# Windowed attention feeding a routed expert layer: routing steps, gathers, buffers and weight loads re-timed

## The chip, the cores and the metric

The kernel runs on one core of a Trainium2 chip. The metric is the time of one execution in device microseconds (us); lower is better. The core has a matrix engine (TensorE, "PE"; its weight loads are listed apart as "PEld"), a vector engine (VectorE, "DVE"), a scalar engine (ScalarE, "ACT"), a general engine (GpSimd, "POOL"), an engine that here does nothing but start transfers (SyncE, "SP"), and 16 DMA engines that move the data. Each engine runs its own instructions strictly in the order in which they stand in its program, and waits at an instruction until everything that this instruction needs is there.

## What is computed

Attention with a sliding window (96 keys back, and 8 global keys at the start), 4 batches of 8 heads, 768 tokens, head size 64; its output, 3072 rows of 512, goes through a layer of 8 experts of which each token takes one.

```
# attention, per batch and head
scores = q @ k.T / sqrt(64) + bias(distance, head)
keep   = (pos_k < 8) | ((0 <= rel) & (rel < 96))
a      = softmax(where(keep, scores, -1e9));  out = a @ v
# x: (3072, 512), the heads side by side
logits = normalise(x) @ normalise(expert_emb).T / tau
e, gate = argmax(logits), softmax(logits)[argmax]
out[n] = gate[n] * (relu(x[n] @ w1[e[n]]) @ w2[e[n]])      # w1: 512x1024, w2: 1024x512
```

## The kernel before

The function `window_attention` (from L376) does the attention and, beside it, the routing: which expert each token takes and at which place of that expert's list of rows it stands. Two heads are one pair, so there are 16 pairs (4 in each batch), and each pair has two halves of 384 tokens. That makes 32 steps, one for each pair and half, counted from 0. Steps 0 to 23 are the first three batches, a pair's two halves one after the other. In steps 24 to 31 the last batch runs half by half: first half 0 of pairs 12, 13, 14 and 15, then half 1 of the same pairs.

A step s does the following, and PE, DVE, ACT and SP run it in the order in which the code is written. For POOL a scheduler sets the order when the program is built.

- `score`: 32 products of keys and queries on PE (L491), then `grow`, the exponential on ACT (L499, L504), and `weigh`, the multiplication with a table of the window and the bias on DVE (L514, L519).
- `turn`: transposes of the next pair's k and q on PE (L448) and copies of them on ACT.
- `turn_x`: the transpose of the finished rows `xs` of the step before on PE (L594), its copy to `xT` on DVE (L595).
- `attend` of step s-1: the products with v on PE (L562). `collect` of step s-1 on DVE: it divides by the sum (L571, L574) and writes into `xs`, a tile of 384 rows of 512 that four pairs fill. When a batch's half is full, `store_x` sends it to `x_dram` on SP (L579). There are three such tiles, used in turn.
- The values v of a pair lie in one of five tiles in turn. SP loads them (L472, L465), and a copy on POOL (L458, `spread_v`) puts the first 8 rows, the global keys, in place for every block. `attend` of the pair needs that copy. SP issues the loads of pair s//2+4: k and q at even s, v at odd s.

The routing of a batch (for the last batch, of each half) is a chain over several steps. `score_experts` (PE L612) and `turn_products` (PE L621, then DVE L622) give the logits `lg`. The generator `choose` then goes on in parts: on DVE the largest logit and the running counts (`m`, `oh`, `cum`, L200 to L212); on PE two small products that count over partitions (L218, L220); on DVE the totals (`both`, `cnt`, L227, L229), the norm (`ss`, L233 to L235), and place and weight of each token (`slot`, `gate`, `mt`, L241 to L255). POOL then scatters `mt` into the table `meta` in DRAM, 128 tokens for each indirect DMA (L259): six for a batch, three for a half. Batch 2 has its `score_experts` at the end of step 25, `turn_products` and the first DVE part in step 26, and the rest in step 27; half 0 of batch 3 has them in steps 29, 30 and 31. Half 1 of batch 3 is routed behind the last `attend`.

Expert 0's first 256 rows are taken from the first three batches, so that their products can start early: `first_rows` loads their entries of `meta` (SP L1011, the tile `emt`) after step 29 and waits for batch 2's scatters; `first_gathers` casts them to row numbers (POOL L683) and fetches the rows with two indirect DMAs (POOL L1021, `xg`) in step 31. `first_turn` transposes them (PE L692) and `first_product` multiplies them with w1 of expert 0 (PE L700).

SP also loads the weights of expert 0 in 32 pieces of 128 KB (L177, 16 of `w1t`, then 16 of `w2t`), from step 20 on: one in each step up to 22, then up to five. After the attention it loads 16 pieces of `w1t` of expert 1, the first of which waits for the gathers. Then it loads the entries of the next block of rows (`mts`, L1738), whose gathers (POOL L1021, `idss`) start the expert loop behind.

PSUM banks for all products but `od` are five tiles in a ring (`bank()`), so an instruction that takes a bank waits until the one five takes earlier is free.

Of the kernel before, what the change touches and what calls it, by code (L numbers as in the profile page):

```python
# [57 lines left out]
def build_route_consts(k):  # L58
    nc, pool = k.nc, k.const

    k.prefix = pool.tile([P, P], F32, name="prefix")
    nc.gpsimd.memset(k.prefix[:], 1.0)
# [4 lines left out]
    nc.gpsimd.iota(k.eidx[:], pattern=[[0, k.NT], [1, k.E]], base=0, channel_multiplier=0,  # L67
                   allow_small_or_imprecise_dtypes=True)
# [3 lines left out]
    nc.gpsimd.iota(k.fills[:], pattern=[[4, CAP // P]], base=0, channel_multiplier=0,  # L72
                   allow_small_or_imprecise_dtypes=True)
    k.wid = pool.tile([P, len(WIDTHS) - 1], F32, name="wid")
    nc.gpsimd.iota(k.wid[:], pattern=[[WIDTHS[-1] - WIDTHS[-2], len(WIDTHS) - 1]], base=WIDTHS[0],
                   channel_multiplier=0, allow_small_or_imprecise_dtypes=True)
# [3 lines left out]
    for i in range(2):  # L80
        nc.gpsimd.iota(k.tok[:, :, i], pattern=[[P, k.B * k.NT]], base=0, channel_multiplier=1,
                       allow_small_or_imprecise_dtypes=True)
    nc.gpsimd.tensor_scalar_add(k.tok[:, last:, 0], k.tok[:, last:, 0], 1.0)
    k.cnt = pool.tile([P, k.E], F32, name="cnt")
    nc.gpsimd.memset(k.cnt[:], 0.0)
    k.good = pool.tile([P, 1], F32, name="good")
    nc.gpsimd.memset(k.good[:], 1.0)
    zrow = pool.tile([P, k.DM // P], F32, name="zrow")
    nc.gpsimd.memset(zrow[:], 0.0)
    k.zrow = zrow  # L90
    k.fill = pool.tile([P, k.SL // P, 3], F32, name="fill")
    nc.gpsimd.memset(k.fill[:, :, 0], float(k.ZR))
    nc.gpsimd.memset(k.fill[:, :, 1], float(k.N))
    nc.gpsimd.memset(k.fill[:, :, 2], 0.0)
# [239 lines left out]
def window_table(k, tmp):  # L334
# [19 lines left out]
    nc.vector.tensor_scalar(out=t[:], in0=rel[:], scalar1=0.0, scalar2=None, op0=ALU.is_lt)  # L354
    yield
# [20 lines left out]
def window_attention(k, ctx):  # L376
# [17 lines left out]
    xt_p, xs_p, rt_p = pool("wa_xt", 2), pool("wa_xs", 3), pool("wa_rt", 2)  # L394
# [5 lines left out]
    values = [const.tile([P, 2, NB, D + 1], F32, name="v%d" % i) for i in range(5)]  # L400
# [42 lines left out]
    def turn(t, i):  # L443
# [5 lines left out]
        if i < 2:  # L449
            nc.scalar.copy(out=t.kT[:, 4 * half : 4 * half + 4, GLB:P],  # L450
                           in_=ps[:, 0:HALF].rearrange("d (j c) -> d j c", c=BLK))
        else:
            nc.scalar.copy(out=t.qT[:, half * HALF : (half + 1) * HALF], in_=ps[:, 0:HALF])
# [171 lines left out]
    def start_half(t, h):  # L625
# [4 lines left out]
        hf.count = 2 if t.b >= B - 2 else 3  # L630
        hf.last = hf.count + (t.b < B - 2)
# [17 lines left out]
    def half_ranks(hf):  # L649

        if hf.router and hf.phase == hf.count:
            hf.router.send(bank()[:, 3 * P :])
            next(hf.router)

    def half_root(hf):

        if hf.router and hf.phase == hf.last:
            next(hf.router)

    def half_router(hf):  # L660

        if hf.router and hf.phase in (1, hf.last):
# [3 lines left out]
        if (hf.t.b, hf.h, hf.phase) == (B - 2, 1, 2):  # L666
            k.base = k.const.tile([P, E], F32, name="base")
            nc.vector.memset(k.base[:], 0.0)
            nc.vector.tensor_scalar(out=k.base[:, 0:1], in0=k.cnt[:, 0:1], scalar1=float(FIRST), scalar2=None, op0=ALU.min)
# [11 lines left out]
    def first_gathers():  # L681
        ids = k.ea.tile([P, FIRST // P, 2], I32, name="ids", tag="ids")
        i = nc.gpsimd.tensor_copy(out=ids[:], in_=k.first.mt[:, :, 0:2])  # L683
        wait_for(k, i, k.root)
# [32 lines left out]
    load_tokens(nc.scalar, first.q, k.q, first, 0)  # L717
    idle = bank()
    nc.vector.memset(idle[:], 0.0)
    build_consts(k)  # L720
# [13 lines left out]
    for t in pairs[1:4]:  # L734
        open_pair(t)
        load_qk(t)
        if t is pairs[1]:
            load_v(first, True)
        load_v(t)
        if t is pairs[2]:  # L740
            emb = prep_expert_emb(k, k.emb_in, k.tau, tmp)
            next(emb)
# [3 lines left out]
    next(table)  # L746
    for v in values:
        nc.gpsimd.memset(v[:, :, :, D : D + 1], 1.0)
    for x in grown:
        nc.gpsimd.memset(x[:, :, :, 2 * BLK :], 0.0)  # L750
    for x in kept:
        nc.gpsimd.memset(x[:, :, BLK:], 0.0)
    next(numbers)
    next(table)
    build_route_consts(k)


    turn(first, 0)
    turn(first, 2)
    busy(1)  # L760
# [12 lines left out]
    for s, (g, p) in enumerate(steps):  # L773
# [6 lines left out]
        if ahead < len(pairs):  # L780
# [3 lines left out]
            else:  # L784
                load_v(pairs[ahead])
# [13 lines left out]
        grow(us[0], 1)  # L799
        if s == 0:  # L800
            turn(first, 3)
            next(table)
        scored = score(us[1])
# [5 lines left out]
        grow(us[1], 0)  # L809
# [14 lines left out]
        if waiting and (s >= 8 * (B - 1) or all(hf.phase >= 1 for hf in active)):  # L824
            active.append(start_half(*waiting.pop(0)))
        if s == len(steps) - 1:
            weigh(us[1])
        for hf in active:
            half_turns(hf)
        for x in whole_xs:  # L830
            turn_x(*x, nc.vector.tensor_copy)
        for hf in active:
            half_ranks(hf)
        if s == len(steps) - 1:
            gathers = first_gathers()
# [3 lines left out]
        weights_part(1 if s < drawn else 3)  # L839
# [14 lines left out]
        for hf in active:  # L854
            if hf.phase == 0:
                score_experts(hf)
            half_router(hf)
            hf.phase += 1
        if s >= len(steps) - 5:
            scatter_later(k, len(k.later))  # L860
# [7 lines left out]
    collect(*steps[-1])  # L868
    turn_x(*steps[-2], nc.scalar.copy)
    first_turn(0)  # L870
# [7 lines left out]
    first_turn(1)  # L878
# [969 lines left out]
```

## Time and profile before

| | us |
|---|---|
| median of 3 runs | 503.98 |
| lowest, highest | 503.79, 506.62 |
| profiled execution, its own time | 504.03 |
| its span, first to last instruction | 501.9 |
| steps 0 to 31 and the last attend, on PE | 6.98 to 158.45 |
| last half's routing and first rows, to the load of `mts` | 158.45 to 182.12 |
| expert loop and end | 182.12 to 501.9 |

The span is 2.1 us shorter than the time of the same execution, which has what lies around it. In the views that follow, a row of the timeline has the start, the duration of the group (us), the engine, the line, the operation, output<-input and how many; in brackets how long the engine stood idle ahead of it and what released it. A row of the waits has the total, the times and the longest, in us. A row of the windows has the stretch and its length, the busy time and number of instructions of PE, PEld, DVE, ACT and POOL, then the mean TensorE clock that was granted (1.00 is full), the DMA share and GB/s. Lines are those of the kernel before; the kernel after has the same code two or three lines further down in most places.

### The profile page before, as it was taken

To read this page: it belongs to the slowest core of one execution; us is meant where nothing else is said; L and a number is where in the kernel's file an instruction comes from. 1 tells how busy PE (TensorE), PEld (TensorE's weight loads), DVE (VectorE), ACT (ScalarE), POOL (GpSimd) and SP (SyncE) were. 2 spreads that over 40 slices of the span, in tenths; PEclk is the share of its full clock that TensorE was granted. 3 is DMA by queue.
4 is the path that set the end of the run, shared out by engine and by line. 5 is a ranking of instruction groups with operands and counts; after the bars stand their busy time and mean duration, and the time that the engine had idled before them with its cause. 6 is when DMAs were issued, how large, how long until landed. Compare 5 with 4: busy or idle time off the path is not lost.

```text
span 501.9 us, 12563 instructions
## 1 busy us (share of the span) xinstructions
PE 473.2 (94%) x4922; PEld 398.6 (79%) x4922; DVE 330.9 (66%) x686; ACT 177.8 (35%) x456; POOL 239.5 (48%) x287
## 2 busy tenths in 40 slices
PE   8899799999797997999999999999999999999995
PEld 6798688888586787879778578888899689869964
DVE  6677587887687555838575825976786765736631
ACT  5776666777663311302112212211221221311210
POOL 6121125225245224376568577666846726854022
PEclk9999999999999798999999999999999999999999
DMA  9999999998863737429561157265175175122001
GB/s 171 196 193 160 233 206 186 225 191 160 256 188 81 174 29 217 140 74 360 198 205 42 54 166 260 89 210 195 51 235 184 42 248 178 39 70 81 0 24 69
DMA packets 112636, 76.31 MB, mean 152 GB/s; under 512 B 88293, under 2 KB 96485, under 8 KB 112497
## 3 DMA queue, kind: packets, MB, share of 16 engines
q1 hardware_dynamic: 103632, 59.22, 47.3%
q0 software_dynamic: 8064, 15.27, 10.1%
q8 instruction: 60, 0.98, 0.9%
q14 instruction: 80, 0.65, 0.4%
q10 hardware_dynamic: 800, 0.20, 0.2%
HBM read 61.67 MB, written 17.16 MB: 157 GB/s over the span
## 4 chain that ended last, share of the span: by engine, by line
PE 69%; DVE 12%; issue 8%; DMA 5%; SPq 3%; POOL 2%; ACT 1%; DVEq 0%; POOLq 0%
PE big L1365 23%; PE big L1171 10%; PE work L1299 7%; PE od L562 6%; PE pa L491 4%; PE pa L700 3%; PE pa L448 3%; PE work L1312 3%; PE big L1342 2%; PE work L1171 2%; PE pa L594 2%; DVE xT L1057 1%; PE work L1090 1%; DVE ex L514 1%; PE pa L612 1%
## 5 line engine op out<-in xcount | busy, mean ns | idle before, releaser
L1048 POOL DMA_INDIRECT xg<-x_dram,squares x96 | 102.9, 1072 | 57.5 <-issue 41.7
L1375 DVE TENSOR_TENSOR hT<-big,hT 128x320 f32<-128x320 f32 (+4 forms) x70 | 39.0, 564 | 51.2 <-PE big L1365 44.8
L1365 PE MATMUL big<-xT,w1t 128*128 128x160 f32 (+4 forms) x336 | 59.4, 330 | 1.2 <-DVE xT L1109 1.2
L1365 PEld LDWEIGHTS big<-xT,w1t 128*128 128x128 f32 x336 | 54.8, 190 | 4.1 <-issue 2.1
L562 PE MATMUL od<-v,ex 128*64 128x65 f32 x1632 | 54.6, 224 | 0.0
L562 PEld LDWEIGHTS od<-v,ex 128*64 128x64 f32 x1632 | 50.3, 138 | 4.4 <-issue 4.2
L499 ACT ACTIVATE ex<-pa 128x384 f32<-128x384 f32 x96 | 42.2, 490 | 32.1 <-PE pa L491 31.8
L259 POOL DMA_INDIRECT meta<-mt,slot x24 | 26.7, 1114 | 46.7 <-PE pa L491 18.6
L491 PE MATMUL pa<-qT,kT 64*64 64x160 f32 (+3 forms) x1024 | 41.7, 288 | 2.1 <-issue 1.7
L1377 ACT ACTIVATE hT<-hT 128x320 f32<-128x320 f32 (+4 forms) x42 | 22.2, 531 | 59.4 <-DVE hT L1375 59.4
L514 DVE TENSOR_TENSOR ex<-ex,table 128x384 f32<-128x384 f32 x72 | 34.4, 519 | 11.8 <-ACT ex L499 10.3
L1365 PE MATMUL big<-xsum,fsum 128*128 128x160 f32 (+4 forms) x224 | 39.8, 331 | 2.1 <-DVE hT L1375 2.1
L491 PEld LDWEIGHTS pa<-qT,kT 64*64 64x64 f32 x1024 | 33.4, 135 | 9.5 <-issue 4.1
L1365 PEld LDWEIGHTS big<-xsum,fsum 128*128 128x128 f32 x224 | 36.4, 190 | 3.8 <-DVE hT L1375 2.6
L1318 POOL DMA_INDIRECT out_dram<-y_arm,tids x17 | 18.6, 1094 | 36.2 <-ACT y_arm L1301 23.7
L1299 PE MATMUL work<-w2t,hT 128*128 128x512 f32 x80 | 35.1, 594 | 0.0
L458 POOL COPY v<-v 32x896 f32<-32x896 f32 x15 | 15.5, 1036 | 37.0 <-DMA v<-in_v_dram 22.1
L519 DVE TENSOR_TENSOR ex<-ex,table 128x768 f32<-128x768 f32 x28 | 27.3, 974 | 9.0 <-ACT ex L499 8.7
L1171 PE MATMUL big<-wsum,hsum 128*128 128x256 f32 x136 | 31.1, 380 | 0.6 <-ACT ptmp L1197 0.5
L1171 PEld LDWEIGHTS big<-wsum,hsum 128*128 128x128 f32 x136 | 25.7, 190 | 5.1 <-issue 0.9
L1299 PEld LDWEIGHTS work<-w2t,hT 128*128 128x128 f32 x80 | 15.1, 190 | 17.6 <-issue 17.6
L1171 PE MATMUL big<-w2t,hT 128*128 128x256 f32 x112 | 27.6, 386 | 1.2 <-DVE hsum L1136 1.2
(240 smaller groups left out, 870.9 us busy)
## 6 DMA issues: line engine op xcount, KB each, us to landing
w1t<-in_moe_w_dram SPq DMA_DIRECT2D x24, 512.0 KB, 6.5
w2t<-in_moe_w_dram SPq DMA_DIRECT2D x6, 2048.0 KB
v<-in_v_dram SPq DMA_DIRECT2D x32, 192.0 KB, 5.5
x_dram<-xs SPq DMA_DIRECT2D x8, 768.0 KB, 6.4
k<-in_k_dram SPq DMA_DIRECT2D x30, 192.0 KB, 4.6
q<-in_q_dram SPq DMA_DIRECT2D x30, 192.0 KB, 5.5
w1t<-in_moe_w_dram SPq DMA_DIRECT2D x32, 128.0 KB, 6.2
w2t<-in_moe_w_dram SPq DMA_DIRECT2D x32, 128.0 KB, 3.3
```

The lines of the kernel that those rows point to most:

```text
L259: i = nc.gpsimd.indirect_dma_start(out=k.meta[:], out_offset=bass.IndirectOffsetOnAxis(ap=slot[:, t : t + 1], axis=0), in_=mt[:, t, :], in ...
L491: i = nc.tensor.matmul(u.sp[e][k0 : k0 + P // 2, x * 2 * BLK + c0 : x * 2 * BLK + c1], lhsT=t.kT[rows, j + x, k0 : k0 + P // 2], rhs=t.qT[ ...
L499: nc.scalar.activation(u.ex[:, e, :, 0 : 2 * BLK], u.sp[e][:, 0 : u.n].rearrange("p (x c) -> p x c", x=2), AF.Exp, scale=k.scale)
L514: nc.vector.tensor_tensor(out=to, in0=src, in1=tab, op=ALU.mult)
L519: nc.vector.tensor_tensor(out=ex, in0=ex, in1=tab, op=ALU.mult)
L562: nc.tensor.matmul(ps[g * SLICE : (g + 1) * SLICE, col : col + D + 1], lhsT=src, rhs=t.v[:, e, j, :], start=g not in begun, stop=True, ski ...
L1048: k.nc.gpsimd.indirect_dma_start(out=xgs[j][:, g * P : (g + 1) * P], out_offset=None, in_=src, in_offset=bass.IndirectOffsetOnAxis(ap=ids[ ...
L1171: i = self.k.nc.tensor.matmul(ps, lhsT=x[:, f, :], rhs=w[:, f, :], start=f == 0 and not add, stop=True, skip_group_check=True)
L1299: nc.tensor.matmul(ps[:], lhsT=hT[:, f, j * P : (j + 1) * P], rhs=w2[:, f, :], start=i == 0, stop=i == k.NF - 1)
L1365: nc.tensor.matmul(to[f // 2][:, f % 2 * 256 : f % 2 * 256 + h], lhsT=x[:, l, f * P : (f + 1) * P], rhs=y[:, l, 0:h], start=not (add or f ...
L1375: nc.vector.tensor_tensor(out=to, in0=x, in1=z, op=ALU.add)
L1377: nc.scalar.activation(to, to, AF.Relu)
```

## The change

It has five parts.

1. **Routing.** For batch 2 and half 0 of batch 3 (`hf.soon`) the first DVE part (`m` to `cum`) follows straight behind the last `xT` copy of the step, ahead of the step's second `weigh` and its `collect`. The two counting products on PE (L218, L220) stand at the end of that same step, behind `attend`, and no longer in the middle of the next one. The rest (`both` to `mt`) is issued in one go at the start of the next step (27, and 31), and the scatters there too, where they stood at its end. `turn_products` stands ahead of the `turn`s.
2. **First rows.** The load of `emt` stands after step 28, the gathers in step 30, both `first_turn`s right behind the last `attend`. A wait of the cast for the square root is taken out. `first_product(1, ...)` is cut after three columns and not after two.
3. **Buffers.** Four tiles of `xs` for three; four of v for five, with the loads of a pair's v issued one pair later.
4. **Weight pieces.** Five each in steps 23 to 25; the 14 that are left (`w2t` of expert 0) after the last `attend`, the first of them waiting for the gathers; then the last `store_x` and the 16 pieces of expert 1.
5. **Opening.** One memset and the constants change places and the memset covers fewer columns; the first copy of q goes from ACT to DVE; one more filler product; in step 0 the third exponential stands ahead of the table's; POOL's memsets and constants wait for an operation of the table on DVE; and SP issues k and q of pairs 1, 2, 3 with v of pairs 0, 1, 2 between them (v of pair 3 in step 1), so that one pair's v fewer lies ahead of the q of pair 2.

The core of the diff:

```diff
-    xt_p, xs_p, rt_p = pool("wa_xt", 2), pool("wa_xs", 3), pool("wa_rt", 2)
+    xt_p, xs_p, rt_p = pool("wa_xt", 2), pool("wa_xs", 4), pool("wa_rt", 2)
-    values = [const.tile([P, 2, NB, D + 1], F32, name="v%d" % i) for i in range(5)]
+    values = [const.tile([P, 2, NB, D + 1], F32, name="v%d" % i) for i in range(HP)]
...
+        hf.soon = t.b >= B - 2
+        hf.count, hf.last = (1, 2) if hf.soon else (3, 4)
...
         if hf.router and hf.phase == hf.count:
             hf.router.send(bank()[:, 3 * P :])
+            if not hf.soon:
+                next(hf.router)
+
+    def half_chain(hf):
+
+        if hf.router and hf.soon and hf.phase == 1:
             next(hf.router)
 
+    def half_slots(hf):
+
+        if hf.router and hf.soon and hf.phase == hf.last:
+            for _ in range(3):
+                next(hf.router)
...
-    for t in pairs[1:4]:
+    for i, t in enumerate(pairs[1:4]):
         open_pair(t)
         load_qk(t)
-        if t is pairs[1]:
-            load_v(first, True)
-        load_v(t)
...
+        load_v(pairs[i], not i)
...
+    signs = next(table)
...
+        wait_for(k, nc.gpsimd.memset(x, what), [signs])
+    build_route_consts(k, signs)
...
-            else:
-                load_v(pairs[ahead])
+        if s % 2 and ahead - 1 < len(pairs):
+            load_v(pairs[ahead - 1])
...
         grow(us[0], 1)
+        for hf in active:
+            half_slots(hf)
...
         if s < len(steps) - 5:
             scatter_later(k, 1, [scored] + k.root)
-        grow(us[1], 0)
+        else:
+            scatter_later(k, len(k.later))
...
         for hf in active:
-            half_ranks(hf)
+            half_chain(hf)
+            if not hf.soon:
+                half_ranks(hf)
+        if s == len(steps) - 2:
+            gathers = first_gathers()
...
-        weights_part(1 if s < drawn else 3)
+        if s < drawn + 3:
+            weights_part(1 if s < drawn else 5)
...
             if hf.phase == 0:
                 score_experts(hf)
+            if hf.soon:
+                half_ranks(hf)
             half_router(hf)
...
-        if s == len(steps) - 3:
+        if s == len(steps) - 4:
             first_rows()
-        weights_part(0 if s < drawn else 2)
...
     collect(*steps[-1])
+    for j, (e, i) in enumerate(weights):
+        wait_for(k, load_weights_part(k, e, k.w[e], i), [] if j else gathers)
...
     for i in range(PIECES // 2):
-        wait_for(k, load_weights_part(k, 1, k.w[1], i), gathers if i == 0 else [])
+        load_weights_part(k, 1, k.w[1], i)
```

How the instructions stand afterwards, at three places. First POOL, from batch 1's scatters (`mt_2013` before, `mt_2008` after) to the gathers. The v tiles are numbered: before, `v_109` is that of pair 15, the last; after, it is `v_112`. Before:

```order
L458 COPY v_112<-v_112 32x2x7x64
L259 DMA meta<-mt_2013,slot_2008 28672x3
L458 COPY v_113<-v_113 32x2x7x64
L259 DMA meta<-mt_2013,slot_2008 28672x3 x2
L458 COPY v_109<-v_109 32x2x7x64
L259 DMA meta<-mt_2013,slot_2008 28672x3
L223 TENSOR_TENSOR ss<-ss,half 128x6
L259 DMA meta<-mt_2527,slot_2522 28672x3 x6
L223 TENSOR_TENSOR ss<-ss,half 128x3
L683 CAST ids<-emt 128x4
L1021 DMA xg<-x_dram,ids 128x512 x2
```

The copy for pair 15 stands ahead of the last scatter of batch 1. After, on the same engine at the same place:

```order
L262 DMA meta<-mt_2008,slot_2003 28672x3 x2
L460 COPY v_111<-v_111 32x2x7x64
L226 TENSOR_TENSOR ss<-ss,half 128x6
L262 DMA meta<-mt_2468,slot_2463 28672x3 x6
L460 COPY v_112<-v_112 32x2x7x64
L697 CAST ids<-emt 128x4
L1044 DMA xg<-x_dram,ids 128x512 x2
```

The copy for pair 15 now stands behind all six scatters of batch 2 (`mt_2468`). Next PE, at the end of step 26 in the kernel after (`od` are the products of `attend`, L564; L493 are the scores of step 27):

```order
L596 MATMUL pa_127<-ident,xs 128x128 x3
L564 MATMUL od<-v_110,ex_115 64x65 x13
L564 MATMUL od<-v_110,ex_116 64x65
L564 MATMUL od<-v_110,ex_115 64x65
L564 MATMUL od<-v_110,ex_116 64x65 x9
L221 MATMUL pa_123<-oh,prefix 128x48
L223 MATMUL pa_123<-cum,ones 128x48
L493 MATMUL pa_124<-qT,kT 64x128
```

Before, the two counting products stood behind the `turn_x` of step 27, ahead of that step's `attend`; now they close step 26. Last, SP from the last v load to the load of `mts`, after:

```order
L474 DMA v_112<-in_v_dram 96x8x64 x2
L467 DMA v_112<-in_v_dram 32x2x64
L180 DMA w1t<-in_moe_w_dram 128x256 x3
L180 DMA w2t<-in_moe_w_dram 128x256 x2
L581 DMA x_dram<-xs 128x3x512
L1034 DMA emt<-meta 128x2x3
L180 DMA w2t<-in_moe_w_dram 128x256 x14
L581 DMA x_dram<-xs 128x3x512
L180 DMA w1t<-in_moe_w_dram 128x256 x16
L1761 DMA mts<-meta 128x4x3 x8
```

Before, all 16 pieces of `w2t` stood ahead of the load of `emt`; now 14 of them stand behind it, and the load of `emt` stands right behind the store of batch 3's half 0, as it did with one piece between.

More of the change, by code (lines that the diff above doesn't have):

```diff
@@ L452, in turn @@
         else:
-            nc.scalar.copy(out=t.qT[:, half * HALF : (half + 1) * HALF], in_=ps[:, 0:HALF])
+            copy(out=t.qT[:, half * HALF : (half + 1) * HALF], in_=ps[:, 0:HALF])
         if i == 0:
@@ L652, in half_ranks @@
             hf.router.send(bank()[:, 3 * P :])
+            if not hf.soon:
+                next(hf.router)
+    def half_chain(hf):
+        if hf.router and hf.soon and hf.phase == 1:
             next(hf.router)
+    def half_slots(hf):
+        if hf.router and hf.soon and hf.phase == hf.last:
+            for _ in range(3):
+                next(hf.router)
+            if hf.t.b == B - 2:
+                k.base = k.const.tile([P, E], F32, name="base")
+                nc.vector.memset(k.base[:], 0.0)
+                nc.vector.tensor_scalar(out=k.base[:, 0:1], in0=k.cnt[:, 0:1], scalar1=float(FIRST), scalar2=None, op0=ALU.min)
     def half_root(hf):
-        if hf.router and hf.phase == hf.last:
+        if hf.router and not hf.soon and hf.phase == hf.last:
             next(hf.router)
     def half_router(hf):
-        if hf.router and hf.phase in (1, hf.last):
+        if hf.router and not hf.soon and hf.phase in (1, hf.last):
             next(hf.router)
@@ L665, in half_router @@
             check_sums(hf.t)
[L666 to L669, printed above, removed]
     def first_base():
@@ L682, in first_gathers @@
         ids = k.ea.tile([P, FIRST // P, 2], I32, name="ids", tag="ids")
-        i = nc.gpsimd.tensor_copy(out=ids[:], in_=k.first.mt[:, :, 0:2])
-        wait_for(k, i, k.root)
+        nc.gpsimd.tensor_copy(out=ids[:], in_=k.first.mt[:, :, 0:2])
         xgs, gathers = gather_rows(k, ids, k.ea2, FIRST // P, k.ZR + 1)
@@ L717, in window_attention @@
     load_tokens(nc.scalar, first.q, k.q, first, 0)
+    build_consts(k)
     idle = bank()
-    nc.vector.memset(idle[:], 0.0)
-    build_consts(k)
+    nc.vector.memset(idle[:, 64:], 0.0)
     warm = const.tile([P, 1], F32, name="warm")
@@ L745, in window_attention @@
     table = window_table(k, tmp)
[L746 to L752, printed above, removed]
+    signs = next(table)
+    for x, what in ([(v[:, :, :, D : D + 1], 1.0) for v in values] + [(x[:, :, :, 2 * BLK :], 0.0) for x in grown] +
+                    [(x[:, :, BLK:], 0.0) for x in kept]):
+        wait_for(k, nc.gpsimd.memset(x, what), [signs])
+    build_route_consts(k, signs)
+    turn(first, 0)
+    turn(first, 2, nc.vector.tensor_copy)
+    busy(2)
     next(numbers)
     next(table)
[L755 to L760, printed above, removed]
     turns = [[] for _ in steps]
@@ L808, in window_attention @@
             scatter_later(k, 1, [scored] + k.root)
-        grow(us[1], 0)
+        else:
+            scatter_later(k, len(k.later))
+        if s:
+            grow(us[1], 0)
+        if waiting and (s >= 8 * (B - 1) or all(hf.phase >= 1 for hf in active)):
+            active.append(start_half(*waiting.pop(0)))
+        for hf in active:
+            if hf.soon:
+                half_turns(hf)
         todo = turns[s]
@@ L823, in window_attention @@
             emb.send(bank() if s == 7 else None)
[L824 to L827, printed above, removed]
         for hf in active:
-            half_turns(hf)
+            if not hf.soon:
+                half_turns(hf)
         for x in whole_xs:
```

64 lines of the change are left out of this document (32 added, 32 removed).

## The prediction

> **What bounds the kernel now.** I read the page's busy times first, then the waits of PE and DVE, then the timeline of the stretches that the change touches.
>
> ```profile
> span 501.9 us, 12563 instructions
> PE 473.2 (94%) x4922; PEld 398.6 (79%) x4922; DVE 330.9 (66%) x686; ACT 177.8 (35%) x456; POOL 239.5 (48%) x287
> ```
> ```profile
> PE pa L491 <- issue: 1.7, 1, 1.7
> ```
> ```profile
> DVE xs L574 <- DMA x_dram<-xs: 3.6, 1, 3.6
> ```
>
> PE is busy for 94% of the span, so what a part of the change is worth is the PE idle time that it takes away or brings. What happens on another engine counts only where PE waits for it. The profiled execution took 504.03 us, 0.05 over the median, and the sum is made against it. All positions below are on the clock of the kernel before.
>
> **A, opening: -1.4.** In step 2 PE waits for the q of pair 2 (first row). The new load order puts one pair's v less ahead of it.
>
> ```profile
> 19.81 0.52 PE L448 MATMUL pa<-ident,q 128*128 128x128 f32 x3 [1.65 <-DMA q<-in_q_dram]
> ```
> ```profile
> 12.00:16.00 4.00, 4.00 (x96) 3.50 (x96) 2.93 (x5) 3.97 (x14) 0.00 (x0) 1.00 1.29 187
> 16.00:20.00 4.00, 2.21 (x47) 1.66 (x42) 2.33 (x6) 3.04 (x8) 0.92 (x1) 1.00 1.27 197
> ```
> ```profile
> v<-in_v_dram SPq DMA_DIRECT2D x32, 192.0 KB, 5.5
> ```
>
> A pair's v is two transfers of 192 KB, 393 KB in all; at the 187 and 197 GB/s of those windows that is 2.0 to 2.1 us, more than the wait of 1.65, which goes. ACT is next late: from 12 to 16 it is busy for 3.97 of 4 us, and the exponential put ahead of the table's there can push a consumer by up to its own half microsecond; the q copy on DVE gives ACT as much back. I take +0.25 of that, and bounds of -1.9 to -1.0. POOL's memsets wait for DVE now, but POOL has nothing in 12 to 16, so I price that, the memset, the filler product and the moved constants inside these bounds. The v loads that come a pair later still come three pairs (six steps) ahead of use, against 5.5 us from issue to landing: nothing.
>
> **B, fourth `xs` tile: -3.0.** DVE stood at L574 for a tile that its store had not yet left, and PE stood behind it:
>
> ```profile
> 60.50 0.56 DVE L574 TENSOR_TENSOR xs<-od,rd 128x384 f32<-128x384 f32 x1 [3.58 <-DMA x_dram<-xs]
> ```
> ```profile
> 61.20 0.52 PE L594 MATMUL pa<-ident,xs 128*128 128x128 f32 x3 [2.63 <-DVE m L200]
> ...
> 66.26 0.52 PE L594 MATMUL pa<-ident,xs 128*128 128x128 f32 x3 [0.65 <-DVE xs L574]
> ```
>
> The two PE gaps are 3.28 us. With a fourth tile the store has a half batch more time; I leave 0.3 for what DVE itself is late with. Bounds -3.3 to -2.6.
>
> **C, batch 2's routing and POOL's order: +7.5.** This is the large term. DVE in steps 26 and 27:
>
> ```profile
> 132.97 0.56 DVE L595 COPY xT<-pa 128x384 f32<-128x384 f32 x1 [0.70 <-PE pa L594]
> 133.45 0.82 DVE L514 TENSOR_TENSOR ex<-ex,table 128x384 f32<-128x384 f32 x2
> ...
> 134.46 0.20 DVE L571 RECIPROCAL rd<-od 128x6 f32<-128x6 f32 x1
> ...
> 135.17 0.19 DVE L200 TENSOR_REDUCE m<-lg 128x6 f32<-128x48 f32 x1
> ...
> 136.56 0.97 DVE L212 TENSOR_TENSOR cum<-cum,oh 128x8 f32<-128x8 f32 x5
> ...
> 138.85 0.21 DVE L227 TENSOR_TENSOR both<-pa,cnt 128x56 f32<-128x56 f32 x1
> ...
> 139.17 0.82 DVE L514 TENSOR_TENSOR ex<-ex,table 128x384 f32<-128x384 f32 x2
> ...
> 140.18 0.17 DVE L233 TENSOR_SCALAR ss<-ss 128x6 f32<-128x6 f32 x1
> ...
> 140.73 0.19 DVE L571 RECIPROCAL rd<-od 128x6 f32<-128x6 f32 x1
> ...
> 141.43 0.20 DVE L241 TENSOR_TENSOR both<-both,oh 128x48 f32<-128x48 f32 x1
> ...
> 142.41 0.19 DVE L255 RECIPROCAL mt<-gate 128x6 f32<-128x6 f32 x1
> ```
>
> And PE:
>
> ```profile
> 132.79 1.62 PE L562 MATMUL od<-v,ex 128*64 128x65 f32 x48
> ...
> 137.58 0.42 PE L220 MATMUL pa<-cum,ones 128*128 128x48 f32 x2 [0.72 <-DVE cum L212]
> ...
> 142.10 1.62 PE L562 MATMUL od<-v,ex 128*64 128x65 f32 x48
> ```
>
> The `xT` copy of step 26 ends at 133.53. The chain from `m` to `cum` takes 2.36 (135.17 to 137.53), so `cum` is ready at 135.9. PE is done with that step's `attend` at 134.41 and waits 1.5 there; behind its wait stand the scores of step 27. In return step 27 loses the wait of 0.72, so the `attend` of step 28 would come at 142.10 + 0.8 = 142.9. On DVE `weigh` and `collect` of step 26 follow the chain (133.45 to 134.46 and 134.46 to 135.17, 1.72 in all), so `both` starts at 137.6. From `both` to the end of `mt` took 3.75 (138.85 to 142.60), of which 1.01 (`weigh`) and 0.70 (`collect`) stood between and do so no more: 2.04, `mt` at 139.65, three microseconds sooner than before. POOL then starts the scatters:
>
> ```profile
> 142.89 1.70 POOL L259 DMA_INDIRECT meta<-mt,slot  x1 [7.07 <-DVE base L669]
> ...
> 150.24 1.37 POOL L259 DMA_INDIRECT meta<-mt,slot  x1 [0.30 <-issue]
> ```
> ```profile
> 58.67 0.92 POOL L458 COPY v<-v 32x896 f32<-32x896 f32 x1 [8.01 <-PE pa L448]
> ```
>
> The six take 8.72 us (142.89 to 151.61), so they end at 148.4. By the new order of POOL the v copy of pair 15 stands behind them: 0.3 + 0.92 more, 149.6. `attend` of step 28 is the first to use this v, and PE waits there with everything behind it. Before, the copy stood ahead of a scatter of batch 1 and was long done. PE stands for 149.6 - 142.9 = 6.7 us, and with the 0.8 the term is +7.5; +6.5 if `mt` comes a microsecond sooner, +8.5 if later.
>
> **D, the clock behind that stall: +2.5.** A PE that stood still got half a clock afterwards:
>
> ```profile
> 163.00:171.00 8.00, 8.00 (x33) 5.55 (x34) 1.84 (x10) 3.13 (x8) 1.43 (x2) 0.61 0.74 154
> 196.00:200.00 4.00, 3.84 (x16) 3.87 (x17) 3.71 (x20) 0.30 (x1) 0.00 (x0) 0.57 0.72 209
> ```
>
> A mean of 0.61 over 8 us is 6.2 us at half (0.39 x 8 / 0.5); 0.57 over 4 is 3.4. A stretch at half clock loses half its length where PE sets the pace: 3.1 or 1.7. I take 2.5, with 0 and 3.4 as ends; 0 because the gap of 2.63 at 61.20 cost nothing, though 6.7 is far longer. The Trainium skill, "TensorE: Matmul & The Clock Gate", Part 1, has a rule that speaks against this change: an idle window of about 3.4 us halves the clock until a busy one has passed. By that rule a wait of 6.7 us all but surely holds such a window, the half clock lasts 3.4 to 6.8 us, and the term is 1.7 to 3.4; without the rule it could be nothing, and the sum would be 502.8.
>
> **E, the same wait at the end of step 30: +0.8.** Batch 3's half 0 has three columns, not six, so its chain is shorter. It lies between 0 and the 1.5 of step 26; I take the middle.
>
> **F and G, the end of the attention: -2.8 and -2.5.**
>
> ```profile
> 156.88 1.57 PE L562 MATMUL od<-v,ex 128*64 128x65 f32 x48
> ```
> ```profile
> 160.84 0.66 PE L692 MATMUL pa<-ident,xg 128*128 128x128 f32 x4 [1.91 <-DMA xg<-x_dram,ids]
> ...
> 162.83 1.12 PE L692 MATMUL pa<-ident,xg 128*128 128x128 f32 x4 [1.01 <-DMA xg<-x_dram,ids]
> 163.88 1.51 PE L612 MATMUL pa<-xT,enb 128*32 128x384 f32 x8
> ```
>
> PE waits 1.91 and 1.01 for the gathered rows. They come sooner than the attention's end in the new order (below), so both go, less 0.1 for the last `xs`: F -2.8, bounds -2.9 to -2.0. With the gap gone the clock stays full, and the 6.2 us at half behind it give back up to 3.1; I take G -2.5, because the logits' way over DVE does not get shorter, and 0 if the clock falls there all the same.
>
> **H and I, small ones: +0.3 and -0.6.**
>
> ```profile
> 181.93 1.89 PE L1171 MATMUL big<-w2t,fhT 128*128 128x256 f32 x8
> ```
>
> The weight pieces that now land while the first products run share the DMA engines with them; PE reads the `w2t` pieces from 181.93 on. I take +0.3, between 0 and 1.5. The wait of 1.7 us at L491 with no releaser may be gone when the code lies elsewhere, which I give a third: -0.6.
>
> **J, SP's queue behind the gathers: +0.5.** 30 pieces stand now between the gathers and the load of `mts`:
>
> ```profile
> 126.33 4.40 SPq L177 DMA_DIRECT2D w1t<-in_moe_w_dram  x5
> ...
> 144.87 0.39 SPq L579 DMA_DIRECT2D x_dram<-xs  x1
> ...
> 154.54 0.38 SPq L1011 DMA_DIRECT2D emt<-meta  x1
> ...
> 162.93 12.11 SPq L177 DMA_DIRECT2D w1t<-in_moe_w_dram  x16
> 182.12 4.86 SPq L1738 DMA_DIRECT2D mts<-meta  x8
> ```
>
> The load of `emt` stands behind the store of batch 3's half 0, which needs the `collect` of the stalled `attend`: 2.77 us after its start before (142.10 to 144.87), some 1.6 more at half clock, and the 0.4 of the store: 149.6 + 4.8 = 154.4. From the issue of `emt` to the landing of the gathers it was 8.3 (154.54 to 162.83): 162.7, and less A and B, 158.3 on the new clock. A piece took 0.757 us (12.11 / 16) or 0.88 (4.40 / 5), so 30 of them are done at 181.0 or 184.7. `mts` is due at 182.12 plus the other terms, about 183. So PE waits between nothing and 1.8 us more.
>
> **Sum:** -1.4 - 3.0 + 7.5 + 2.5 + 0.8 - 2.8 - 2.5 + 0.3 - 0.6 + 0.5 = +1.3, so 504.03 + 1.3 = 505.3. What is gained at three places is given back at one.
>
> **Rivals.**
>
> R1, no stall: the copy is through POOL before PE needs it, so C is +0.8 and D is 0. That is 505.3 - 6.7 - 2.5 = 496.1. For it: the order is a list and not a time, and the 8.72 us rest on one row of six scatters. Against it: POOL takes what stands first, and the scatters start only with `mt`. To be 1% faster the copy must end by about 145. Chance 0.13.
>
> R2, slower: SP's queue takes over. If the gathers land 2.2 us later than I say (160.5) and a piece takes 0.88, `mts` comes at 186.9, 3.9 later than due and, beyond the 0.5 already in, that is 508.7; with a landing where it was before (162.8) it is 511. Middle 509.8. It decides from a landing of about 159 at 0.88 a piece. For it: four steps hang one behind the other (stall, `collect`, store, `emt`). Against it: before, 16 pieces left SP idle for five microseconds ahead of `mts`. Chance 0.17.
>
> R3, the change doesn't do what it says: the loads set the attention's pace, so a wait taken out comes back at the next transfer, and A and B give nothing: 505.3 + 4.4 = 509.7. For it: a DMA share over 1 from 12 to 20. Against it: that falls behind the opening. Chance 0.05.
>
> **How the numbers follow.** The forecast has 0.65, its own range is 501 to 509.5: C by 1, D and G by up to 2.5 each, not all one way. R2 and R3 lie up to 511, R1 at 496.1. From 498.5 to 511 about 0.83 is held; R1's middle is left out. About 1% (5.0 us) can be told from no change. Under 498.9: R1 and a little of the forecast's lower end, 0.15. Over 509.0: two thirds of R2 and R3, and the upper end of the forecast, 0.18. Within: 0.67.
>
> **What would show it.** C: in step 28 PE idle for 5 to 8 us ahead of L564, released by POOL's copy behind six scatters. D: a clock of 0.5 for 3 to 7 us behind it. A and B: no wait for q in step 2, none for the store of `xs`, `score` of step 24 about 4.4 sooner than before. F, G: no wait for `xg` behind the last `attend`, and full clock there. J: SP goes from the last piece into the load of `mts` without idling. The prediction is wrong if PE does not stand in step 28, or if `mts` comes later than 185.

## The result

The changed kernel takes 509.14 us (median of 20 runs, 505.18 to 515.15), the kernel before 503.65 on the same chip (20 runs, 500.56 to 510.24). The ratio is 1.0105, 95% interval 1.0076 to 1.0133: slower by about 1%. The ratio is taken over the runs in the chip's faster state alone, so it is not exactly the quotient of the medians. The prediction said 505.3 with a range of 498.5 to 511.

The page of the changed kernel has a longer span, PE busy for a slightly smaller share of it, and a different chain of work that ended last. First three lines of the kernel after (span, busy times, the chain by engine), then the chain by engine of the kernel before:

```profile
span 508.1 us, 12564 instructions
PE 474.0 (93%) x4924; PEld 397.6 (78%) x4924; DVE 330.2 (65%) x687; ACT 177.4 (35%) x455; POOL 243.8 (48%) x286
PE 49%; issue 16%; DMA 13%; POOL 13%; DVE 4%; POOLq 2%; SPq 1%; ACT 1%; ACTq 0%; DVEq 0%
```
```profile
PE 69%; DVE 12%; issue 8%; DMA 5%; SPq 3%; POOL 2%; ACT 1%; DVEq 0%; POOLq 0%
```

PE works about as long as before (474.0 against 473.2), so 5.4 of the 6.2 us of span are waiting. On the chain POOL and DMA went from 2% and 5% to 13% each: the gathers that POOL issues stand on it. Most of that is not in step 28, where the prediction looked. The shares alone do not price anything, though: a version below that is faster than the kernel before (opening and buffers alone) has POOL at 17% and DMA at 11%.

Where the time stands on PE's clock in the two profiled executions (504.03 and 510.48 us):

| mark | before | after | difference |
|---|---|---|---|
| score of step 3 | 22.13 | 20.30 | -1.8 |
| score of step 13 | 68.63 | 63.52 | -5.1 |
| score of step 26 | 127.16 | 124.57 | -2.6 |
| end of the last attend | 158.45 | 162.76 | +4.3 |
| counting products of the last half done | 170.78 | 169.96 | -0.8 |
| load of `mts` | 182.12 | 185.21 | +3.1 |
| first 160-column product of the expert loop | 196.16 | 198.84 | +2.7 |
| first 192-column product | 373.51 | 374.36 | +0.9 |
| first 240-column product | 410.90 | 415.66 | +4.8 |
| last group of products | 494.20 | 500.46 | +6.3 |

Four stretches matter. In step 28 PE stops where the prediction said. PE's timeline of the kernel after, then POOL's, then the clock over the whole stretch and over the two microseconds in which it falls and comes back:

```profile
139.17 0.56 PE L564 MATMUL od<-v,ex 128*64 128x65 f32 x10
144.22 2.43 PE L564 MATMUL od<-v,ex 128*64 128x65 f32 x38 [4.49 <-POOL v L460]
146.58 2.03 PE L493 MATMUL pa<-qT,kT 64*64 64x128 f32 x32
```
```profile
135.55 1.31 POOL L262 DMA_INDIRECT meta<-mt,slot  x1 [3.94 <-DVE base L670]
...
142.27 0.96 POOL L262 DMA_INDIRECT meta<-mt,slot  x1 [0.30 <-issue]
143.23 0.94 POOL L460 COPY v<-v 32x896 f32<-32x896 f32 x1
```
```profile
136.00:150.00 14.00, 8.26 (x146) 7.27 (x144) 6.52 (x15) 4.03 (x15) 6.64 (x7) 0.76 0.32 77
141.00:142.00 1.00, 0.00 (x0) 0.00 (x0) 0.00 (x0) 0.00 (x0) 0.96 (x1) 0.79 0.04 5
148.00:149.00 1.00, 1.00 (x18) 0.90 (x11) 0.35 (x2) 1.00 (x4) 0.00 (x0) 0.79 0.57 215
```

The copy of pair 15's v runs behind the sixth scatter, and `attend` resumes as it ends. A mean clock of 0.76 over 14 us is 6.7 us at half. A mean of 0.79 in a microsecond is 0.42 us at half, so the clock falls at about 141.6, 1.9 us into the wait, and is back at about 148.4. Some 2.6 us of the half clock fall into the wait and the rest on work: the two groups behind the wait take 2.43 and 2.03.

At the attention's end the waits for the gathered rows are gone, and all is caught up:

```profile
161.01 1.75 PE L564 MATMUL od<-v,ex 128*64 128x65 f32 x48
162.82 0.55 PE L596 MATMUL pa<-ident,xs 128*128 128x128 f32 x3
163.20 1.04 PE L705 MATMUL pa<-ident,xg 128*128 128x128 f32 x8
164.08 0.49 PE L596 MATMUL pa<-ident,xs 128*128 128x128 f32 x3
164.50 1.55 PE L614 MATMUL pa<-xT,enb 128*32 128x384 f32 x8
```

No group has an idle time in brackets. Up to the counting products the change is ahead by 0.8 us. Then it loses. SP's and POOL's timeline of the kernel after, and the wait of SP's queue (in this part of the kernel the lines of the kernel after stand 23 further down: L1761 is L1738 before):

```profile
167.18 13.20 SPq L180 DMA_DIRECT2D w1t<-in_moe_w_dram  x16
185.21 4.55 SPq L1761 DMA_DIRECT2D mts<-meta  x8
```
```profile
175.84 0.96 POOL L262 DMA_INDIRECT meta<-mt,slot  x1 [0.30 <-issue]
189.04 1.25 POOL L1044 DMA_INDIRECT xg<-x_dram,idss  x1 [12.23 <-issue]
```
```profile
SPq L1761 <- DMA meta<-mt,slot: 3.6, 1, 3.6
```

SP is done with the pieces at 180.38 and then waits for the scatters, the last of which POOL had finished at 176.80. From there to the load of `mts` it is 8.4 us; before it was 4.7 (177.39 to 182.12). While the pieces move, the scatters land later. This reaches PE by way of DVE, which stands at the conversion of `mts` with a sum behind it (`hsum`) that PE needs. DVE and PE of the kernel after, then DVE of the kernel before at the same place, where PE did not wait:

```profile
188.06 0.17 DVE L1765 CAST idss<-mts 128x16 int32<-128x16 f32 x1 [5.13 <-DMA mts<-meta]
```
```profile
188.88 3.33 PE L1194 MATMUL big<-wsum,hsum 128*128 128x256 f32 x8 [2.12 <-DVE hsum L1156]
```
```profile
184.83 0.18 DVE L1742 CAST idss<-mts 128x16 int32<-128x16 f32 x1 [0.65 <-DMA mts<-meta]
```

Behind this wait of 2.12 the clock is at half for another 3.4 us (a mean of 0.76 from 187 to 194).

The last loss is far behind, in the expert loop. PE of the kernel after, and DVE at the same place:

```profile
374.36 2.76 PE L1388 MATMUL big<-xT,w1t 128*128 128x192 f32 x16
379.01 2.87 PE L1388 MATMUL big<-xsum,fsum 128*128 128x192 f32 x16 [1.89 <-DVE fsum L1158]
383.37 2.87 PE L1388 MATMUL big<-xT,w1t 128*128 128x192 f32 x16 [1.49 <-ACT hT L1412]
```
```profile
373.43 1.10 DVE L1080 STREAM_TRANSPOSE xT<-xg 128x512 f32<-128x512 f32 x1 [5.22 <-DMA xg<-x_dram,squares]
```

DVE waits 5.22 us for rows that a POOL gather brings, and PE for DVE. POOL's queue has fallen back: the first gather for these rows starts at 339.99 here and started at 323.86 before (next two rows, after and before), while PE is one microsecond apart.

```profile
339.99 0.99 POOL L1071 DMA_INDIRECT xg<-x_dram,squares  x1 [9.23 <-issue]
```
```profile
323.86 1.27 POOL L1048 DMA_INDIRECT xg<-x_dram,squares  x1 [3.49 <-issue]
```

### The profile page after: what moved, and what is told of

The parts are those of the page before. It is cut to its first block, busy times and chain, and to the rows that moved or that the text cites. A ratio compares the mean times of both kernels' runs of the same rounds, so it can differ in the third digit from the quotient of the medians.

```text
span 508.1 us, 12564 instructions
## 1 busy us (share of the span) xinstructions
PE 474.0 (93%) x4924; PEld 397.6 (78%) x4924; DVE 330.2 (65%) x687; ACT 177.4 (35%) x455; POOL 243.8 (48%) x286
## 4 chain that ended last, share of the span: by engine, by line
PE 49%; issue 16%; DMA 13%; POOL 13%; DVE 4%; POOLq 2%; SPq 1%; ACT 1%; ACTq 0%; DVEq 0%
DMA xg<-x_dram,squares 11%; PE big L1388 10%; PE od L564 9%; POOL xg L1071 6%; PE pa L493 6%; PE big L1194 5%; PE pa L450 4%; POOL out_dram L1341 4%; PE pa L713 3%; PE work L1322 3%; PE pa L596 2%; PE big L1365 2%; PE work L1335 2%; PE work L1113 1%; POOLq L1836 1%
## 5 line engine op out<-in xcount | busy, mean ns | idle before, releaser
L1071 POOL DMA_INDIRECT xg<-x_dram,squares x96 | 106.6, 1110 | 63.0 <-issue 48.0
L564 PE MATMUL od<-v,ex 128*64 128x65 f32 x1632 | 56.3, 226 | 4.7 <-POOL v L460 4.5
L564 PEld LDWEIGHTS od<-v,ex 128*64 128x64 f32 x1632 | 51.7, 140 | 9.5 <-issue 4.8
L493 PE MATMUL pa<-qT,kT 64*64 64x160 f32 (+3 forms) x1024 | 42.4, 290 | 2.3 <-issue 2.0
L493 PEld LDWEIGHTS pa<-qT,kT 64*64 64x64 f32 x1024 | 34.1, 136 | 9.6 <-issue 4.2
L1194 PE MATMUL big<-wsum,hsum 128*128 128x256 f32 x136 | 32.6, 393 | 2.6 <-DVE hsum L1156 2.1
L1080 DVE STREAM_TRANSPOSE xT<-xg 128x512 f32<-128x512 f32 x24 | 24.9, 1082 | 10.0 <-DMA xg<-x_dram,squares 9.2
```

Of the source, the lines that this page charges most:

```text
L493: i = nc.tensor.matmul(u.sp[e][k0 : k0 + P // 2, x * 2 * BLK + c0 : x * 2 * BLK + c1], lhsT=t.kT[rows, j + x, k0 : k0 + P // 2], rhs=t.qT[ ...
L564: nc.tensor.matmul(ps[g * SLICE : (g + 1) * SLICE, col : col + D + 1], lhsT=src, rhs=t.v[:, e, j, :], start=g not in begun, stop=True, ski ...
L1071: k.nc.gpsimd.indirect_dma_start(out=xgs[j][:, g * P : (g + 1) * P], out_offset=None, in_=src, in_offset=bass.IndirectOffsetOnAxis(ap=ids[ ...
L1194: i = self.k.nc.tensor.matmul(ps, lhsT=x[:, f, :], rhs=w[:, f, :], start=f == 0 and not add, stop=True, skip_group_check=True)
```

## The experiments

Ratios are to the kernel before on the same chip; its medians were 501.59 (first four), 501.95 (next four) and 512.06 (last four).

**Copy ahead of the scatters.** All scatters from step 27 on wait for the last `spread_v`, so POOL runs the copy first (the core of the edit; `k.spread` is set to that copy).

```diff
-            scatter_later(k, len(k.later))
+            scatter_later(k, len(k.later), [k.spread])
```

> The changed kernel with one thing undone: batch 2's scatters wait for the v copy of pair 15, so the copy stands ahead of them on POOL. Theory (the copy behind the scatters costs the stall of step 28 and half a clock behind it, and nothing else hangs on it): PE's wait of 4.49 us for POOL's copy is gone and the two groups behind it (2.43 and 2.03 us where 1.62 and 1.16 are usual) are back to size, together about 6 us in step 28, so about 503 us. Rival (the last weight pieces, which run into the next stage, set the time from there on): the load of mts stays near 185 and the time moves by less than 2 us, 507 to 509.

505.24 us, ratio 1.0077 (1.0044 to 1.0111), which overlaps with that of the changed kernel. The stall of step 28 is gone, but another has come, at the last `attend`. PE, DVE and POOL of this kernel:

```profile
157.03 2.87 PE L564 MATMUL od<-v,ex 128*64 128x65 f32 x48 [4.53 <-DVE ex L521]
```
```profile
154.44 0.17 DVE L236 TENSOR_SCALAR ss<-ss 128x3 f32<-128x3 f32 x1 [4.35 <-POOL ss L226]
```
```profile
150.33 0.19 POOL L697 CAST ids<-emt 128x4 int32<-128x4 f32 x1 [5.27 <-DMA emt<-meta]
151.21 1.01 POOL L1044 DMA_INDIRECT xg<-x_dram,ids  x1 [0.69 <-POOL ids L697]
152.52 0.97 POOL L1044 DMA_INDIRECT xg<-x_dram,ids  x1 [0.30 <-issue]
153.51 0.90 POOL L226 TENSOR_TENSOR ss<-ss,half 128x3 f32<-128x3 f32 x1
```

The change has a second such order. The square root of half 0 (`ss`, POOL) stands behind the cast and the gathers, which wait for `emt`; DVE waits for the root, with the `weigh` behind it that PE needs. In the changed kernel the first stall covers this. The theory was right about the stall and wrong that nothing hung on it.

**Weight pieces as before.** `weights_part(1 if s < drawn else 3)` and two more at the step's end, and the 16 pieces of expert 1 behind the gathers.

> The changed kernel with the weight pieces issued as before (three and two in each step from 23 on, 16 pieces of expert 1 behind the gathers). Theory that the pieces slow the landing of the last scatters, and with it the gathers behind them and POOL's queue in the expert loop: the load of mts comes within 6 us of the last scatter's end and not 8.4, POOL's first gather of the loop no longer 12 us after it, and the loop behind it loses its waits; 509.1 less 3 to 8 us, 501 to 506. Rival (the loop's waits come from how POOL's gathers fall between the expert weights' transfers, whatever happened ahead of it): the load of mts comes sooner, the time moves by under 2 us.

503.21 us, 1.0054 (1.0012 to 1.0096), some 2.5 us under the changed kernel's ratio, though the two intervals overlap. `mts` is loaded 4.6 us behind the last scatter's end (179.99 against 175.37), so the landing is quick again. The stall of step 28 is there as before, with the same length:

```profile
142.33 2.43 PE L564 MATMUL od<-v,ex 128*64 128x65 f32 x38 [4.50 <-POOL v L460]
```

**Both edits.**

> Both edits: copy ahead of the scatters and weight pieces as before, so of the change the routing, the buffers and the opening are left. If both theories hold: no stall in step 28, the load of mts at about 175, 494 to 498 us. If only the stall counts: about 503, as with the copy alone. If only the pieces count: about 504.

497.35 us, 0.9920 (0.9876 to 0.9963). Against the kernel with the weight pieces alone mended only the copy's place differs: 1.34% of 501.59, 6.7 us, give or take 3 by the two intervals, for the stall and the clock behind it. Here POOL's scheduler also put the root ahead of the cast, so the second stall does not come. PE in step 28 runs through:

```profile
137.22 0.52 PE L596 MATMUL pa<-ident,xs 128*128 128x128 f32 x3 [1.24 <-DVE xs L576]
137.67 1.62 PE L564 MATMUL od<-v,ex 128*64 128x65 f32 x48
139.22 1.16 PE L493 MATMUL pa<-qT,kT 64*64 64x128 f32 x32
```

and `mts` comes at 174.94, 4.1 us behind the last scatter.

**Opening and buffers alone**, with the copy ahead of the scatters; `hf.soon = False`, first rows and pieces as before.

> Opening and buffers of the change alone (four tiles of xs and of v, v a pair later), with the copy of pair 15 ahead of batch 2's scatters; routing, first rows and weight pieces as in the kernel before. By the sum of the prediction A and B are 4.4 us (499.3); in the trace of the changed kernel the score of step 3 comes 1.8 us sooner and that of step 26 2.6 us, so 501.0. Rival (loads set the attention's pace, what is gained at one wait comes back at the next): 503 to 504.

499.16 us, 0.9934 (0.9888 to 0.9981). The routing that the version above has besides is worth nothing that these two can show.

**Copy and root first, weight pieces of the change.** `first_gathers` is called at the end of step 30 and its cast waits for the root again.

> The changed kernel with both orders of POOL mended: pair 15's copy ahead of batch 2's scatters, and the square root of half 0 ahead of the cast and the gathers of the first rows. With the copy alone in front the stall of 4.49 us in step 28 went, but PE stood 4.53 us at the last attend, because DVE waited 4.35 us for the square root behind the gathers. Theory A (these two waits on POOL are what the change costs): the second goes too, 5 to 6 us less than with the copy alone, so a ratio to the kernel before of 0.995 to 0.998. Theory B (the weight pieces behind the gathers hold the landing of the last scatters and so the load of mts): the attention ends 5 us sooner, the load of mts and the gathers of the next block come less than 2 us sooner, PE waits there instead, and the ratio stays at 1.003 to 1.008.

503.59 us, 1.0019 (0.9985 to 1.0052). Between the two theories: the attention ends at 153.98 (159.90 with the copy alone), but `mts` only goes from 180.77 to 178.86, 7.6 us behind the last scatter. SP and POOL of this kernel:

```profile
166.59 10.98 SPq L180 DMA_DIRECT2D w1t<-in_moe_w_dram  x16
178.86 4.76 SPq L1762 DMA_DIRECT2D mts<-meta  x8
```
```profile
169.61 1.61 POOL L262 DMA_INDIRECT meta<-mt,slot  x1 [0.30 <-issue]
```

Of 5.9 us won in the attention 1.9 arrive at `mts`, the number of theory B but only in part for its reason. PE waits 0.85 and 0.76 for the gathered rows here and then works at half clock (0.51 from 158 to 161), so at the counting products only 2.5 us are left; the landing takes another 0.7. Without both stalls the change is level with the kernel before, not ahead.

**Routing and first rows alone**, on the kernel before, root first.

> Routing and first rows of the change alone, on the kernel before (its opening, its three tiles of xs and five of v, its weight pieces), with the square root ahead of the gathers. By the prediction's terms for it (0.8 for the wait in step 26, 0.8 in step 30, -2.8 and -2.5 at the end of the attention) it is 3.7 us faster, ratio 0.993. Rival, read from the two experiments that differ only in it (spans 494.2 with it, 492.8 without): it gains nothing, ratio 1.000 to 1.004, because the waits that it brings and the scatters that land later behind the pieces take up what it saves.

501.57 us, 0.9996 (0.9956 to 1.0036). The rival holds: routed a step sooner gains nothing. In the profile the gathers of the first rows still hold PE for 0.81, the counting products wait 0.79 in step 26 and `turn_x` 1.24 in step 28; it also has a wait of 3.44 without a releaser, at 130.25. This version has five v tiles, and in it the last copy runs at 124.94, long ahead of the scatters at 140.93: the new routing alone does not put the copy behind them.

**The kernel before, and the changed kernel, once more.**

> The kernel before once more, for a second profile. If the length of the expert loop (from its first 160-column product to its last product, 298.0 us in the first profile) belongs to the kernel, it is within 1 us of that; if it depends on how POOL's gathers fall between the weight transfers in one execution, it may be up to 302.

> The changed kernel once more, for a second profile. The attention, the stall in step 28 and the load of mts 8 us behind the last scatter should come back within 1 us. The expert loop took 301.6 us; if that belongs to the kernel it is 301 to 302 again, if it is chance it may be 298.

496.70 and 507.32 us, one run each. The changed kernel repeats what counts: a wait of 4.49 in step 28, `mts` 7.2 us behind the last scatter, a loop of 302.3 us. The kernel before does not repeat two things on which the prediction stood. DVE's wait of 3.58 for the store of `xs` is not there; the same place in this second profile:

```profile
59.12 0.56 DVE L574 TENSOR_TENSOR xs<-od,rd 128x384 f32<-128x384 f32 x1
```

nor is the wait of 1.7 at L491. So its attention ended at 154.18, four microseconds sooner than in the first profile.

**Three tiles of `xs`** in the version with opening and buffers alone.

```diff
-    xt_p, xs_p, rt_p = pool("wa_xt", 2), pool("wa_xs", 4), pool("wa_rt", 2)
+    xt_p, xs_p, rt_p = pool("wa_xt", 2), pool("wa_xs", 3), pool("wa_rt", 2)
```

> Opening and buffers alone, as in the experiment with ratio 0.993, but with three tiles of xs instead of four. Theory (the fourth tile is worth the 3.3 us that the first profile of the kernel before showed): ratio 1.000 and a wait of DVE for the store of xs of some 3 us near 60 us. Rival (that wait comes only in some executions: a second profile of the kernel before has none): at most 1 us between the two, ratio 0.993 to 0.997, the gain being the opening's 1.8 us and what the loads' order brings.

511.48 us, 0.9980 (0.9932 to 1.0028), on a chip on which all was slower. In its profile the wait is there:

```profile
58.81 0.56 DVE L576 TENSOR_TENSOR xs<-od,rd 128x384 f32<-128x384 f32 x1 [3.39 <-DMA x_dram<-xs]
```

So with three tiles it came in two of four profiles (the kernel before and this one; not in its repetition, nor in the routing alone), and with four in none. What the fourth tile is worth on the mean the intervals do not tell.

**Three kernels once more**, on that chip.

> The version with copy and weight pieces mended once more, beside the others on one chip, for the time (0.992 before) and for a second profile of its expert loop (297.4 us in the first). If the loop's length hangs on the late weight pieces, it is 296 to 299 again, and POOL's gathers stay less than 166 us behind its start at the last gather of the 192-column expert's rows; if it is chance, it may be 301 or more.

> The changed kernel with the weight pieces as before, once more, for a second profile. Its loop took 300.2 us in the first. If late pieces alone lengthen the loop, that was chance and it is 296 to 299 now; if the attention's late end also does, 300 again.

> Opening and buffers alone once more, for a second profile. The loop took 299.3 us in the first; if late pieces alone lengthen it, 296 to 299.

Copy and weights mended: 513.00 us, 1.0041 (1.0000 to 1.0081); one run each of 516.79 and 509.44. What was 0.8% faster on one chip is not faster on another. In the first of these profiles PE stops and starts in step 28 for a reason that no releaser tells:

```profile
138.11 1.67 PE L564 MATMUL od<-v,ex 128*64 128x65 f32 x31
140.46 0.39 PE L564 MATMUL od<-v,ex 128*64 128x65 f32 x2 [0.67 <-issue]
...
143.30 0.50 PE L564 MATMUL od<-v,ex 128*64 128x65 f32 x4 [0.92 <-issue]
```

and the clock is at half for 10 us, from 138.5 to 148.8; it had fallen before the first of these gaps, so they did not set it off. The copy was through at 134.5, so this is another wait, and like the 1.7 at L491 it has no releaser. The wait of step 28 with the copy behind the scatters is 4.49 on this chip too (weights back).

**The expert loop**, from its first 160-column product to its last group, over all profiles:

| kernels | loop, us | load of `mts` behind the last scatter, us |
|---|---|---|
| before, twice | 298.0, 296.2 | 4.7, 4.1 |
| routing alone | 296.6 | 5.0 |
| copy and weights mended | 297.4 | 4.1 |
| opening and buffers | 299.3 | 3.9 |
| weights back | 300.2 | 4.6 |
| changed, twice | 301.6, 302.3 | 8.4, 7.2 |
| copy first | 301.2 | 7.0 |
| copy and root first | 302.9 | 7.6 |
| slow chip: weights back, three `xs`, copy and weights, opening and buffers | 312.2, 309.2, 306.9, 306.0 | 3.8, 7.3, 4.1, 8.2 |

On the faster chips all four executions with late pieces have the long loop and the late `mts`. But the loop with the weights back has 300.2, and on the slow chip every loop is long and `mts` is late twice without the late pieces of the change. So the loop's length hangs on more than the pieces.

The landing of the scatters is another matter: all fourteen profiles go one way. Where SP had issued its last piece 1.6 to 3.1 us before POOL was through with the last scatter, `mts` came 3.9 to 5.0 us behind it (eight profiles). Where SP was still issuing 0.8 to 6.4 us after that, it took 7.0 to 8.4 us (six). The two late ones on the slow chip have their pieces in the old place, but there the last of them was issued 0.8 us after the last scatter.

## Why the prediction was right, and where it was not

The range held the time; the point was 4 us low: +1.3 was forecast and +5.5 came. By one of the two conditions in its last sentence the prediction was wrong: `mts` came at 185.21 in the first profile, past the 185 that it named (181.28 in the second). Two more of its signs did not come: the wait of step 28 is 4.49 and not 5 to 8, and `score` of step 24 is 2.3 us sooner (114.82 against 117.09) and not 4.4. That the time lies inside is in part luck, for the range reached so far up for R2, whose cause, SP still issuing pieces, did not hold `mts` up. The mechanism that carried the sum, POOL's new order, is shown: the wait of step 28 is in each of the four profiles that have that order (4.49, 4.50, 4.49, 4.49; in three the trace names the copy as the releaser), and goes when only the copy's place changes.

- **A, -1.4:** -1.8 at step 3, with a new wait of 0.77 for a q at 11.67 already in it. In all fourteen profiles step 3 starts at 20.2 to 21.0 with the new opening and at 22.1 to 24.1 with the old one. That v loads come six steps ahead of use does not hold for pair 15: its v is issued at 128.94, in step 26, for step 28. PE did not pay for it, but with the copy in front POOL waits 4.84 us for this load (copy first).
- **B, -3.0:** from step 3 to step 13 the changed kernel is 3.3 us faster in these two profiles. But that term was read from one execution; the kernel before has the wait only sometimes. And of the 5.1 us that the change is ahead at step 13, 2.8 are lost again by step 24, 1.6 of them in a wait without a releaser.
- **C, +7.5:** mis-sized. The wait is 4.49 where 6.7 stood. Three things make up the 2.2. The scatters took 7.68 (135.55 to 143.23) and not 8.72, as four of six needed 0.96. Ten of the 48 products of `attend` ran ahead of the wait, in 0.56. And `attend` of step 28 came 3.9 us behind `mt` (135.26 to 139.17) and not 3.25, held 1.24 at `turn_x` where it was 0.53 before.
- **D, +2.5:** about 2.0. The 38 products took 2.43 where 48 take 1.62, the scores 2.03 where they take 1.16. The half clock lasted 6.7 us, but 2.6 of them passed in the wait. Together C's wait and D are 6.5, and the experiment that differs in nothing else gives 6.7, give or take 3. The Trainium skill, "TensorE: Matmul & The Clock Gate", Part 1, has the clock halved by an idle window of about 3.4 us. The trace agrees on the length, two such windows of half clock. It does not show that a whole window must be idle: the clock fell 1.9 us into the wait, and it was at half for 3.4 us behind waits of only 1.75 (before, from 196.6) and 2.12 (after, from 189.4).
- **E, +0.8:** 0.5 (0.32 and 0.16) at the counting products. What I did not see is that the root came to stand behind the gathers on POOL. I followed POOL's queue for the copy and not for the root, though the diff takes that very wait out. It cost nothing only because the first stall covered it.
- **F and G, -2.8 and -2.5:** from the end of the last `attend` to the last half's scores 1.74 us where it was 5.43, so -3.7; from there to the end of the counting products 5.46 where it was 6.90, so -1.4. Together 5.1 where 5.3 stood; that the parts were off by about 1 us, one each way, is hidden by the total.
- **H, +0.3:** not seen. The first products with `w2t` take 1.89 as before (180.68 and 181.93).
- **I, -0.6:** did not come. The wait without a releaser moved, 1.63 us at 102.16 and not 1.71 at 129.95.
- **J, +0.5:** the step that failed. I counted how long SP is busy issuing pieces, and took `mts` to be due when the scatters were issued as before. SP was through in time, at 180.38; what came late was the landing of the scatters, 8.4 us and not 4.7, beside pieces still on the DMA engines (their share is 0.96 from 175 to 180, and was 0.43 before). That is R2's outcome with another holder. PE pays 2.12 us behind DVE for it and then works at half clock. The version with both stalls mended still has it: 7.6 us, and 1.98 of PE behind `hsum`.
- **What the sum left out:** it took everything behind `mts` to shift as one piece. The loop was longer by 3.6 us in these profiles (301.6 against 298.0). In the stretch shown POOL's gathers had no slack left; that this is all of the 3.6 is not shown.

By ratios on one chip: with both mended 0.992, with the copy behind the scatters 1.0054, with the late pieces too about 1.0105 (from another set of runs): -0.8%, +1.3%, +0.5%. By these intervals the first two are clear of the noise and the last is not.

What stays open: why the loop's gathers fall back further in some kernels than in others. The profiles show that they do, that POOL waits for landings between weight transfers, and that PE pays once POOL is late enough; they do not show what sets it off. No kernel was tried that gives POOL fewer gathers there. Nor is a version settled that beats both: copy and weights mended, and opening and buffers alone, beat the kernel before on one chip (0.9920, 0.9934), and the first of them did not on another (1.0041). By their ratios both are under the changed kernel (1.0105), but on the second chip the first of them is so only by overlapping intervals, and the changed kernel was not run there.

## What to carry to other kernels

When an engine's order is left to a scheduler, compare the whole queue before and after for every item that another engine waits for: here one buffer less put a copy, and one wait less a square root, behind transfers that issue one by one. Work moved behind a point does not only queue on its issuer; what it moves can slow the landing of small transfers that the next stage waits for (here 7.0 to 8.4 us and not 3.9 to 5.0), so ask what is in flight then. And a wait that stands in one profile may not be in the next: take a second profile before a term of 3 us is built on it.

## What had not been expected of the hardware

The load that waits for the last indirect scatter started 3.9 to 5.0 us after POOL was done with it where SP had issued its pieces of 128 KB by then, and 7.0 to 8.4 us where it was still issuing them (fourteen profiles).

PE stood still without any releaser at different places in different executions, for 1.0 to 3.4 us, and on the slow chip in crumbs of 0.2 to 0.9, once spread over 7 us. The single waits of 1 us and more in the attention have something in common. Counted in the trace with its weight loads and its own semaphore and register instructions, PE stands at instruction 5057 in the kernel before (1.71 us) and in the routing alone (3.44), at 4033 in the kernel after (1.63) and at 5314 with copy and root first (1.02). These lie 1024 and 257 apart, to within one a multiple of 256. That would fit instructions that come in blocks of 256 and come late; no run tests it, and the crumbs on the slow chip do not lie on this grid.

And the kernel before took 501.6 to 503.7 us in three sets of runs and 512.06 in a fourth, on another chip, where the expert loop was 306 to 312 us long in each of four profiles of other versions.
